# Mamba-2 scan and ELU feed-forward on one Trainium2 core: words of y in shared buffers and two groups sooner, decays begun at a stage's end, copies and B's loads elsewhere

## Chip, core and metric

One NeuronCore of a Trainium2 chip runs the kernel in one launch. The metric is the device time in microseconds (us). Before the change: 357.75 us, the median of three runs (357.48 to 358.91).

The core has five engines that run their own queues in order: TensorE (PE, with its weight loads as PEld), VectorE (DVE), ScalarE (ACT), GpSimd (POOL) and SyncE (SP, which here issues nearly all DMAs). They meet through semaphores, and each buffer is waited for by whoever takes it next.

## What is computed

A state-space scan over 4 batches, 8 heads and 768 tokens (head dimension 32, state 16), then a feed-forward layer with ELU (256 to 2048 to 256) on its output.

```python
for c in range(nc):                       # chunks of 32 tokens
    cum = np.cumsum(la, axis=-1)          # la = log(clip(a, 1e-6, 1))
    L = np.exp(cum[:, :, :, None] - cum[:, :, None, :]) * causal
    M = np.einsum('bhin,bhjn->bhij', Cc, Bc) * L
    y[:, :, sl] = (np.einsum('bhij,bhjd->bhid', M, xc)
                   + np.einsum('bhin,bhnd->bhid', Cc, state) * np.exp(cum)[..., None])
    decay_from_j = np.exp(cum[:, :, -1:] - cum)
    Bx = np.einsum('bhjn,bhjd->bhjnd', Bc, xc) * decay_from_j[:, :, :, None, None]
    state = np.exp(np.sum(la, axis=-1))[:, :, None, None] * state + np.sum(Bx, axis=2)
x = y.transpose(0, 2, 1, 3).reshape(3072, 256)
h = x @ w_in                              # 3072 x 2048
out = np.where(h > 0, h, np.exp(np.minimum(h, 0)) - 1) @ w_out
```

## The kernel before, in words

**Tiling.** The 3072 tokens are twelve groups of 256 (`NP` = 12). From group 2 on, groups are handled in pairs n, n+1 with n = 2, 4, 6, 8, 10, so that one matmul has 512 columns. The scan uses chunks of 64 tokens and works on the pair m = n+2 while the feed-forward works on pair n.

**Words.** From the pair 2 on, the products are made from operands split in two words each: for `h`, w1 and w0 of w and y1 and y0 of y, with a third product of sums (`both`), so three passes of two matmuls (`l1_words`, L828). After them ACT scales `both` into `e` (L834), DVE joins the two (L841), ACT makes ELU's two steps (`begin_end`, L848 and L849), and DVE the result g (`end_words`, L855). For the second product each tile of g is split by a job of three steps: ACT the high word (L909), DVE the low one (L910), POOL their sum (L887), begun, continued and ended by `first_of_jobs`, `second_of_jobs` and `third_of_jobs`. The second product itself (`second`, L968) takes six matmuls of 256 columns per step. For the first pairs it is `l2` (L873), whose result is copied by ACT into `ob` and written out.

**Stages.** The last loops run over n = 4, 6, 8, 10 ("stages"), each over k = 0 to 15, the sixteen column groups of w_in. In a step k the order written out by hand is: job to begin, `l1_words(n, k)`, loading of the words of w for k+4 (k even, `load_words`, 768 KB), the scan's part of that step (`stage_scan`), ELU, the jobs' third step, then so many steps of `second(n-2)` as the list after `l2s` says. Ahead of them lies a loop over j = 8 to 15 (i = j-8) for pair 2, in which the words of w and w_out are also made (`words_of_w`, `low_of_w`, `words_of_out`, `low_of_out`) and pair 4 is scanned.

**The scan in a stage.** For the pair m: `decay_sums` (POOL, L531, one instruction on 128x1024) adds the running sums, `decay_exps` (ACT, L538, two halves), `decay_mask` (POOL, L544, two selects for each half); `turn_part` transposes C and B (DVE), masks heads (part 2, POOL L476) and scales (part 3, POOL L459); `scaled` weights B's tokens (POOL, L423); at k = 9 to 13 come `scores`, `weigh`, `sums`, `states`, `across` and `inside`, and `inside` copies y from PSUM into yT (L687 on DVE, L689 on ACT), once for t = 0 and once for t = 1. SP loads x at k = 2 (`load_x`), B and C for two pairs ahead at k = 6 and 7 (`load_bc`), the decays' sums at k = 11 (`spread_cum`) and B by tokens at k = 12 (`load_b`).

**The end of a stage.** At k = 15 `l1_words` also makes the next pair's words of y: `high_of_y` (y1, one half on ACT L789, one on DVE L793), `low_of_y` (y0, two DVE instructions L802) and `both_of_y` (two, L812). y1 and y0 have one buffer each. The next stage's first group takes the passes on y1 and y0 first and the one on `both` last.

**Buffers.** `big` (4 KB a partition, 26 of them) holds the raw weights, g, the words of g, w and w_out. `small` (2 KB, 17 of them) holds the merged weights w_in and w_out, low words, `ob` and `eo`. A new tile takes the buffer that was freed longest ago in the order of the program, and waits until its last reader is done. PSUM has seven banks for all (`p_a`) and one more (`p_o`), in which `l2` and part of the scan accumulate.

Of the kernel before, what the change touches and what calls it, by code (L numbers as in the profile page):

```python
# [17 lines left out]
P = 128  # L18
# [6 lines left out]
BIG, SMALL = 26, 17  # L25
# [8 lines left out]
def kernel(  # L34
# [627 lines left out]
    def inside(y, *ns, t=None):  # L662

        for t in range(2) if t is None else (t,):
# [16 lines left out]
            for v in range(2):  # L681
                k = shift(n, v)
                for at in (0, k) if k else (0,):
                    count, src = P - k, (at + k) % P
                    to, src = out[at:at + count, :, :, Q * v:Q * v + Q], y[t][v][src:src + count]
                    if t and n == 1:
                        nc.vector.tensor_copy(to, src)  # L687
                    else:
                        nc.scalar.copy(out=to, in_=src)  # L689
# [96 lines left out]
    def high_of_y(n):  # L786
        y = yT[n // 2].rearrange("p k b u i -> p k (b u i)")
        y1 = conv.tile([P, KC, 2 * BLK], F32R, tag="y1", name="y1", bufs=1)
# [8 lines left out]
    def low_of_y(n):  # L797
        y = yT[n // 2].rearrange("p k b u i -> p k (b u i)")
        y1, = y_words[n]
        y0 = conv.tile([P, KC, 2 * BLK], F32R, tag="y0", name="y0", bufs=1)  # L800
# [16 lines left out]
    def l1_words(n, m, ahead=None):  # L817
# [13 lines left out]
        if ahead:  # L831
            high_of_y(ahead)
# [5 lines left out]
        if ahead:  # L838
            low_of_y(ahead)
            both_of_y(ahead)  # L840
        nc.vector.scalar_tensor_tensor(  # L841
            out=high, in0=high, scalar=WORD - 1.0, in1=e, op0=ALU.mult, op1=ALU.add)
        second_of_jobs()
        late.append((n, m, high, e))
# [20 lines left out]
    def l2(n, j, half=None):  # L865
# [11 lines left out]
        if j == MC // 2 - 1 and half != 0:  # L877
            ob = small([P, 2, DM], F32, "ob")
# [12 lines left out]
    def words_of_out(i):  # L891
# [3 lines left out]
        out_words[i] = small([P, 2, DM], F32R, "o_low"), words[:, 0], words[:, 1]  # L895
# [5 lines left out]
    def low_of_out(i):  # L901
        sub(out_words[i][0], pieces[DF // CW + i][0], out_words[i][1].bitcast(F32))
# [306 lines left out]
    for j in range(2 * DIRECT):  # L1209
# [44 lines left out]
        if j == 6:  # L1254
            words_of_w(5)
            low_of_w(5)
            keep_words(4)
    for j in range(8, 16):
# [48 lines left out]
        if i == 6:  # L1307
            decay_sums(6)
# [10 lines left out]
    def stage_scan(n, k):  # L1319
# [9 lines left out]
        if 0 < k < 5:  # L1329
            decay_exps(m + (k > 2), (k - 1) % 2)  # L1330
        if k == 0:
            decay_sums(m + 1)
        if 2 < k < 7:
            decay_mask(m + (k > 4), (k - 3) % 2)
        if k in (2, 7):
            turn_part(m + (k > 2), 2)
        if k in (8, 9):
            scaled(m + k - 8, nc.gpsimd)
        if k == 10:
            turn_part(m, 3)  # L1340
            turn_part(m + 1, 3)
        if k in (6, 7) and m + 2 < NP:
            load_bc(m + k - 4)
        if k in (11, 12) and m + 2 < NP:
            for to in (m + 2, m + 3):
                (spread_cum if k < 12 else load_b)(to)
        if k == 14 and m + 2 < NP:
            decay_sums(m + 2)

    for n in range(4, NP, 2):  # L1350
# [12 lines left out]
        for k in range(16):  # L1363
# [6 lines left out]
            l1_words(n, k, m if k == 15 else None)  # L1370
# [13 lines left out]
            l2s((2 - (n == 4 and k < 1), 2, 2, 2, 2, 2, 2, 2, 2, 2, 2, 2, 2, 1, 1, 0)[k])  # L1384
# [16 lines left out]
        if m:  # L1401
            l2s(2)
# [48 lines left out]
```

## Time and profile before

| what | value |
|---|---|
| median of 3 runs | 357.75 us |
| profiled execution, its own time | 359.41 us |
| its span in the profile | 357.70 us |
| mean granted TensorE clock | 0.995 |
| stage n = 4: first L828 to that of n = 6 | 119.76 to 174.90 us |
| stage n = 6 | 174.90 to 229.91 us |
| stage n = 8 | 229.91 to 284.07 us |
| stage n = 10 | 284.07 us to about 331 us |

The page of the profile lists the busy time of each engine, the chain of work that ended last, and groups of instructions with the idle time ahead of them. The table of waits has, for each pair of waiting line and line waited for, the total in us, how often, and the longest. A row of the timeline has its start, its length, the engine and line, the operation, output and inputs, how many were merged (x), and in brackets how long the engine idled before it and what released it. The ends of matmuls are modelled, so the distance between starts is the better measure of TensorE's pace.

### The profile page before, as it was taken

The page shows a single profiled execution, that of the slowest core. Times are in us where ns is not written, and L with a number is a line of the kernel's source. Part 1 is how long each engine was busy: PE and PEld are TensorE (multiplying, and loading weights), DVE is VectorE, ACT ScalarE, POOL GpSimd, SP SyncE. Part 2 cuts the span into 40 slices and gives each one's busy share as a digit, 9 for nine tenths or more (in the row PEclk, how much of TensorE's full clock was granted, in tenths as well). Part 3 has the DMA queues.
Part 4 walks back from the last instruction along what each step waited for, and adds up shares of the span by engine and source line. Part 5 has one row for each costly group of instructions (what it writes and reads, how often), then busy time and mean ns, then how long its engine had stood idle before and what let it go on. Part 6 is the DMA issues. An engine that isn't in the chain of part 4 may idle for free.

```text
span 357.7 us, 9627 instructions
## 1 busy us (share of the span) xinstructions
PE 342.2 (96%) x3742; PEld 290.0 (81%) x3742; DVE 282.3 (79%) x502; ACT 262.7 (73%) x542; POOL 213.9 (60%) x242
## 2 busy tenths in 40 slices
PE   8889999996999999998999999999999999999996
PEld 6569888884888788886688788788788789999996
DVE  3898989886697867794799987699887587998951
ACT  4698989694858898765689856689866688997601
POOL 5553554538757795976178977368986144876100
PEclk9999999999899999999999999999999999999999
DMA  8899989372468494538138669329364035250001
GB/s 140 206 226 188 283 159 254 71 152 89 164 122 307 186 267 166 197 91 173 75 101 203 216 229 218 100 79 242 150 225 161 2 107 200 88 198 0 32 0 59
DMA packets 82950, 54.79 MB, mean 153 GB/s; under 512 B 59033, under 2 KB 68569, under 8 KB 82905
## 3 DMA queue, kind: packets, MB, share of 16 engines
q1 hardware_dynamic: 80728, 53.98, 54.3%
q8 instruction: 29, 0.48, 0.6%
q10 hardware_dynamic: 2176, 0.20, 0.5%
q14 instruction: 17, 0.13, 0.1%
HBM read 44.53 MB, written 9.63 MB: 151 GB/s over the span
## 4 chain that ended last, share of the span: by engine, by line
PE 57%; DVE 15%; ACT 9%; POOL 9%; issue 5%; SPq 2%; DMA 2%; DVEq 0%; POOLq 0%; ACTq 0%
PE ps_o L968 11%; PE ps_h L828 10%; PE ps_o L873 9%; PE ps_h L711 9%; PE ps_w L828 5%; PE ps_both L968 5%; DVE ps_h L841 4%; DVE g_low L910 3%; POOL g_words L887 3%; POOL L L544 3%; PE ps_y L672 2%; ACT e L849 2%; ACT e L848 2%; DVE y L802 2%; DMA w<-in_moe_w_in_dram 2%
## 5 line engine op out<-in xcount | busy, mean ns | idle before, releaser
L887 POOL TENSOR_TENSOR g_words<-g_words,g_low 128x512 fp32r<-128x512 f32 x62 | 84.8, 1371 | 65.8 <-ACT e L848 40.4
L968 PE MATMUL ps_o<-o_words,g_words 128*128 128x256 f32 x448 | 84.3, 285 | 1.1 <-POOL g_words L887 0.8
L968 PEld LDWEIGHTS ps_o<-o_words,g_words 128*128 128x128 f32 x448 | 72.5, 190 | 8.7 <-POOL g_words L887 4.4
L848 ACT ACTIVATE e<-ps_h 128x512 f32<-128x512 f32 x72 | 43.0, 598 | 37.4 <-DVE ps_h L841 37.3
L855 DVE SCALAR_TENSOR_TENSOR g<-e,ps_h 128x512 f32<-128x512 f32 x72 | 49.3, 684 | 20.7 <-ACT e L849 18.2
L841 DVE SCALAR_TENSOR_TENSOR ps_h<-ps_h,e 128x512 f32<-128x512 f32 x72 | 49.9, 694 | 18.5 <-ACT e L834 15.7
L968 PE MATMUL ps_o<-o_low,g_low 128*128 128x256 f32 x224 | 63.2, 282 | 0.0
L910 DVE SCALAR_TENSOR_TENSOR g_low<-g_words,g 128x512 fp32r<-128x512 f32 x72 | 61.3, 857 | 0.0
L828 PE MATMUL ps_w<-y_both,w_words 128*128 128x512 f32 x144 | 50.7, 429 | 0.7
L873 PE MATMUL ps_o<-w_out,g 128*128 128x256 f32 x192 | 47.2, 391 | 3.4 <-ACT ob L879 3.4
L834 ACT ACTIVATE e<-ps_w 128x512 f32<-128x512 f32 x72 | 42.1, 585 | 7.7 <-PE ps_w L828 7.1
L711 PE MATMUL ps_h<-yT,w_in 128*128 128x256 f32 (+1 forms) x208 | 45.2, 368 | 2.3 <-POOL w_in L254 2.3
L849 ACT ACTIVATE e<-e 128x512 f32<-128x512 f32 x72 | 45.5, 632 | 2.3
L828 PE MATMUL ps_h<-y,w 128*128 128x512 f32 x144 | 46.2, 397 | 0.8 <-DVE y L802 0.4
L828 PE MATMUL ps_h<-y,w_words 128*128 128x512 f32 x144 | 45.9, 400 | 0.7 <-DVE M L586 0.7
L873 PEld LDWEIGHTS ps_o<-w_out,g 128*128 128x128 f32 x192 | 37.0, 195 | 9.4 <-ACT ob L879 3.7
L909 ACT ACTIVATE g_words<-g 128x512 fp32r<-128x512 f32 x72 | 43.6, 623 | 0.0
L711 PEld LDWEIGHTS ps_h<-yT,w_in 128*128 128x128 f32 x208 | 36.3, 190 | 8.3 <-POOL w_in L254 3.4
L968 PEld LDWEIGHTS ps_o<-o_low,g_low 128*128 128x128 f32 x224 | 42.6, 190 | 0.0
L828 PEld LDWEIGHTS ps_h<-y,w 128*128 128x128 f32 x144 | 27.0, 188 | 9.4 <-DVE y L802 2.7
L828 PEld LDWEIGHTS ps_h<-y,w_words 128*128 128x128 f32 x144 | 26.2, 188 | 9.3 <-PE ps_w L828 1.9
L828 PEld LDWEIGHTS ps_w<-y_both,w_words 128*128 128x128 f32 x144 | 23.8, 192 | 5.5 <-DVE y_both L812 3.3
(135 smaller groups left out, 547.7 us busy)
## 6 DMA issues: line engine op xcount, KB each, us to landing
w_words<-w_kept SPq DMA_DIRECT2D x28, 512.0 KB
w<-w_kept SPq DMA_DIRECT2D x28, 256.0 KB
L<-flat SPq DMA_DIRECT2D x20, 256.0 KB
w<-in_moe_w_out_dram SPq DMA_DIRECT2D x8, 512.0 KB
w_kept<-w_words SPq DMA_DIRECT2D x8, 512.0 KB
w<-in_moe_w_in_dram SPq DMA_DIRECT2D x7, 512.0 KB
xr<-in_x_dram SPq DMA_DIRECT2D x24, 128.0 KB
out_dram<-eo SPq DMA_DIRECT2D x18, 128.0 KB
```

Of the source, the lines that this page charges most:

```text
L711: nc.tensor.matmul(out=ps[:, j, toks], lhsT=w_in[i][:, k, j * P:(j + 1) * P], rhs=yT[n // 2][:, k, n % 2].rearrange("p u i -> p (u i)")[:, ...
L828: nc.tensor.matmul(out=ps, lhsT=lhs[:, k], rhs=rhs[:, k], start=k == 0 and lhs is not w0, stop=k == KC - 1 and lhs is not w1)
L834: nc.scalar.activation(e, both, ACT.Copy, scale=WORD)
L841: nc.vector.scalar_tensor_tensor(out=high, in0=high, scalar=WORD - 1.0, in1=e, op0=ALU.mult, op1=ALU.add)
L848: nc.scalar.activation(e, high, ACT.Relu, scale=-1.0)
L849: nc.scalar.activation(e, e, ACT.Exp, scale=-1.0)
L855: nc.vector.scalar_tensor_tensor(out=g_tile(n, m // 2)[:, m % 2].rearrange("p b i -> p (b i)"), in0=e, scalar=1.0, in1=h, op0=ALU.subtract ...
L873: nc.tensor.matmul(out=o_of[n][:, ts], lhsT=g_of[n // 2, j][:, m % 2, n % 2, ts * P:(ts + 1) * P], rhs=w_out[j][:, m % 2], start=(m == 0 a ...
L887: nc.gpsimd.tensor_tensor(out=out, in0=in0, in1=in1, op=ALU.subtract)
L909: yield nc.scalar.activation(words[:, 0], g, ACT.Copy, scale=NEAR / WORD)
L910: yield nc.vector.scalar_tensor_tensor(out=low, in0=words[:, 0].bitcast(F32), scalar=WORD, in1=g, op0=ALU.mult, op1=ALU.subtract)
L968: nc.tensor.matmul(out=ps, lhsT=lhs, rhs=rhs, start=lhs is both_g and first > 0 or lhs is g1 and first > 1, stop=last and lhs is not g1, s ...
```

## The change

y1 and y0 take buffers from `big`, which has 28 instead of 26. `high_of_y` and `low_of_y` for the next pair are made at k = 14 instead of 15, `both_of_y` at k = 15 behind L841. `decay_sums` of the next pair is issued at k = 13 and 14, the first `decay_exps` at k = 15, the other three at k = 0 to 2 of the next stage, `decay_mask` at k = 0 to 3; the masks of heads at k = 4 and 5, `scaled` at 7 and 8. `load_b` goes from k = 12 to k = 3 and 5 of the stage that uses it. From pair 6 on the t = 1 copies of `inside` are made by DVE. `ob` is taken from `big`, and `o_low` is taken when it is written. One step of `second` moves from k = 12 to the stage's end.

```diff
-BIG, SMALL = 26, 17
+BIG, SMALL = 28, 17
...
-                    if t and n == 1:
+                    if t and (n == 1 or n > 4):
                         nc.vector.tensor_copy(to, src)
                     else:
                         nc.scalar.copy(out=to, in_=src)
...
-        y1 = conv.tile([P, KC, 2 * BLK], F32R, tag="y1", name="y1", bufs=1)
+        y1 = big([P, KC, 2 * BLK], F32R, "y1")
...
-        y0 = conv.tile([P, KC, 2 * BLK], F32R, tag="y0", name="y0", bufs=1)
+        y0 = big([P, KC, 2 * BLK], F32R, "y0")
...
-        if ahead:
-            high_of_y(ahead)
         e = ffn.tile([P, 2 * BLK], F32, tag="e", name="e", bufs=2)
         nc.scalar.activation(e, both, ACT.Copy, scale=WORD)
         first_of_jobs()
         if late:
             end_words()
-        if ahead:
-            low_of_y(ahead)
-            both_of_y(ahead)
+        if ahead and m == MC - 2:
+            high_of_y(ahead)
         nc.vector.scalar_tensor_tensor(
             out=high, in0=high, scalar=WORD - 1.0, in1=e, op0=ALU.mult, op1=ALU.add)
+        if ahead and m == MC - 1:
+            both_of_y(ahead)
         second_of_jobs()
+        if ahead and m == MC - 2:
+            low_of_y(ahead)
...
-            ob = small([P, 2, DM], F32, "ob")
+            ob = big([P, 2, 2, DM], F32, "ob")[:, 0]
...
-        out_words[i] = small([P, 2, DM], F32R, "o_low"), words[:, 0], words[:, 1]
+        out_words[i] = None, words[:, 0], words[:, 1]
...
     def low_of_out(i):
+        out_words[i] = small([P, 2, DM], F32R, "o_low"), *out_words[i][1:]
...
+    def begin_decays(m, k):
+
+        if k < 15:
+            decay_sums(m + k - 13)
+        else:
+            decay_exps(m, 0)
+
...
-        if i == 6:
-            decay_sums(6)
+        if i > 4:
+            begin_decays(6, i + 8)
...
-        if 0 < k < 5:
-            decay_exps(m + (k > 2), (k - 1) % 2)
-        if k == 0:
-            decay_sums(m + 1)
-        if 2 < k < 7:
-            decay_mask(m + (k > 4), (k - 3) % 2)
-        if k in (2, 7):
-            turn_part(m + (k > 2), 2)
-        if k in (8, 9):
-            scaled(m + k - 8, nc.gpsimd)
+        if k < 3:
+            decay_exps(m + (k > 0), (k + 1) % 2)
+        if k < 4:
+            decay_mask(m + (k > 1), k % 2)
+        if k in (4, 5):
+            turn_part(m + k - 4, 2)
+        if k in (7, 8):
+            scaled(m + k - 7, nc.gpsimd)
...
+        if k in (3, 5) and n > 4:
+            load_b(m + (k > 3))
...
-        if k in (11, 12) and m + 2 < NP:
+        if k == 11 and m + 2 < NP:
             for to in (m + 2, m + 3):
-                (spread_cum if k < 12 else load_b)(to)
-        if k == 14 and m + 2 < NP:
-            decay_sums(m + 2)
+                spread_cum(to)
+        if k > 12 and m + 2 < NP:
+            begin_decays(m + 2, k)
...
-            l1_words(n, k, m if k == 15 else None)
+            l1_words(n, k, m)
...
-            l2s((2 - (n == 4 and k < 1), 2, 2, 2, 2, 2, 2, 2, 2, 2, 2, 2, 2, 1, 1, 0)[k])
+            l2s((2 - (n == 4 and k < 1), 2, 2, 2, 2, 2, 2, 2, 2, 2, 2, 2, 1, 1, 1, 0)[k])
...
         if m:
-            l2s(2)
+            l2s(3)
```

## Prediction

> **What bounds the kernel now.** I read the page first. TensorE is busy 96% of the 357.7 us span, so what counts is where it stands still or runs slowly; the other engines matter only through that. The table of waits says who makes it stand.
>
> ```profile
> PE   342.2 (96%) x3742; PEld 290.0 (81%) x3742; DVE 282.3 (79%) x502; ACT 262.7 (73%) x542; POOL 213.9 (60%) x242
> ...
> ACT ob L879 <- POOL w L887: 5.0, 1, 5.0
> ...
> PEld ps_o L968 <- POOL g_words L887: 4.4, 9, 0.8
> ...
> PE ps_o L873 <- ACT ob L879: 3.4, 1, 3.4
> ```
>
> One wait of 3.4 us stands out, and its cause is another wait: ScalarE's output copy waited 5.0 us for POOL. The timeline shows it, and the table by stretches the clock (its last three columns: granted clock, DMA share, GB/s).
>
> ```profile
> 83.14 0.61 ACT L767 ACTIVATE w_words<-w_in 128x512 fp32r<-128x512 f32 x1
> 87.31 1.40 POOL L887 TENSOR_TENSOR w<-w_in,w_words 128x256 fp32r<-128x256 f32 x2
> 88.75 0.59 ACT L879 COPY ob<-ps_o 128x512 f32<-128x512 f32 x1 [4.99 <-POOL w L887]
> ...
> 85.90:89.50 3.60, 0.20 (x2) 0.11 (x2) 0.08 (x1) 0.75 (x2) 2.67 (x4) 1.00 0.19 73
> 89.60:92.90 3.30, 3.30 (x9) 2.59 (x9) 2.17 (x4) 3.02 (x9) 1.31 (x2) 0.50 0.79 290
> ```
>
> ob needs no data of POOL's L887. It needs a "small" buffer, and the one that comes free is w_in[5]'s, whose last reader is that L887. TensorE idles, and is then granted half its clock for 3.3 us. Three further places, from the timeline of TensorE: the end of a stage (first two rows), a stop put down to issue (third), and POOL late with g_words (fourth).
>
> ```profile
> 175.98 1.10 PE L828 MATMUL ps_h<-y,w 128*128 128x512 f32 x2 [0.45 <-DVE y L802]
> 177.18 1.10 PE L828 MATMUL ps_w<-y_both,w_words 128*128 128x512 f32 x2
> ...
> 169.21 0.71 PE L672 MATMUL ps_y<-M,xr 64*32 64x64 f32 x48 [1.74 <-issue]
> ...
> 202.69 0.51 PE L968 MATMUL ps_o<-o_words,g_words 128*128 128x256 f32 x2 [0.41 <-POOL g_words L887]
> ```
>
> **1. ob to the big buffers.** The two L828 matmuls at 85.08 are followed by L873 4.31 us later, undisturbed 0.45 (93.83 to 94.28); 0.2 of that is another wait, so 3.7 lost. The eight L873 at half clock take 3.08 (89.39 to 92.47) against 1.54 (94.28 to 95.82), the next pair 0.89 against 0.65: 1.8 more. Together 5.5. The new ob needs a free big buffer: at that point 12 g tiles, two word tiles of w and y's two hold 16 of 28, and the last raw weight was freed by POOL's L254 at 80.95. So ob can run when its matmuls end, near 84.3, 0.59 long, before TensorE asks for the bank near 85.5. What is late next: the low words of w (POOL, done 88.71) are wanted at 95.82 - 5.5 = 90.3; POOL's mask for the scores was held up by the same ACT queue, would end near 88.7 + 1.4 + 1.35 = 91.5 and is wanted at 97.5 - 5.5 = 92.0. Both fit, narrowly. Bounds 3.7 to 5.5; I take **-5.4**, as the half clock follows the idle stretch directly. The two later ob waited for TensorE at most 0.3: nothing.
> [...]
>
> **2. B's loads.** Now four loads of 64 KB are issued at k = 12 of a stage: SyncE spends 7.09 us on them from 160.02. TensorE's stop of 1.74 us lies at 167.47. In the DMA records a 16 KB packet of the instruction queue q8 starts at 166.92 and ends at 167.87, amid the loads' 64-byte packets (164.9 to 169). I read the stop as code that came late behind them. Moved to k = 3 and 5 of the next stage the loads leave this place; the same place of the two later stages shows no stop. Bounds 0 to 1.9; taken **-1.4**.
> The price: at k = 3 and 5 SyncE's queue is full. In stage n = 6 it issues from 183.17 to 207.5 almost without a pause, x's four loads alone 6.37 us (188.43), then the words of w for k = 8 at 194.9, whose packets are in by about 199.2 while TensorE begins k = 8 at 200.74: 1.5 us spare. B's two loads in front add 1.0 to 3.5 us (pairs of 1.01 and 1.14 at 99.15 and 102.90; 7.09 for four). Stage n = 8 has some 3 us spare. scaled() on POOL, at k = 7 and 8, wants B near then. Cost 0 to 2 in n = 6, 0 to 1 in n = 8; taken **+0.7**. n = 4 keeps its early loads.
>
> **3. Decays begun at the stage's end.** Per stage POOL does the same: two sums (L531, 1.95 each), eight selects (L544), ctm, scaling. The selects move from k = 3 to 6 to k = 0 to 3. A pair of selects and a job make 1.84 + 1.30 = 3.14 us against TensorE's 2.82 a step (stage n = 10: k = 3 begins at 294.04, k = 4 at 296.86), so four such steps lag 1.3. Before, with ctm behind them, this ended in late g_words: L968 comes 0.70 and 1.02 after the last L828 pair instead of 0.46 at 199.20 and 202.69, and 0.72, 0.72, 1.02 in n = 8: 0.80 + 1.08 = 1.9 us. Now the lag begins where the third filler group of part 4 (0.72) gives POOL time, and ctm follows a step later. Bounds 0 to 1.9; taken **-1.5**. The exps (0.62 on ACT) move to k = 15 to 2: ACT idles 2.5 to 3.2 us there, so they are hidden.
>
> **4. y's words two groups sooner.** At the end of stage n = 4 the matmul pairs start at 174.90, 175.98, 177.18 and TensorE goes on at 178.12: 1.08, 1.20, 0.94 instead of 0.47 each, 1.8 lost; 1.1 each in n = 6 (pairs at 230.41 and 231.61) and n = 8. With y1 and y0 in own buffers no matmul must end first. But VectorE makes most of it, in order. In n = 6: L841 of k = 14 at 226.77, L910, L793, L855, two L802, two L812, done at 232.16, hardly a pause. After the change the t = 1 copies of inside come to it (three of about 0.4: TensorE's L672 ends near 224.9, so 224.95 to 226.2), then L855 of k = 13 that waited behind them, L793, L841, L910, two L802, L855, L841, two L812: 226.2 + 0.6 + 0.5 + 0.6 + 0.7 + 1.3 + 0.6 + 0.6 + 1.25 = 232.35. So y_both is ready no sooner; y1 and y0 are, by 1 us. Third filler group at the end: +0.72 there, but taken from k = 12, where it covers the wait for Sx (POOL L629 ends 220.99; the products L654 begin 220.49 now and would begin 219.77), so it gives nothing on balance. What stays is the first pair's wait: 0.6 in n = 4, 0.3 in n = 6 and n = 8. Bounds -0.6 to 4.0 of gain; taken **-1.2**. L841 of k = 15 now stands before y_both and is 1.2 sooner, so the banks and eo that hold TensorE 0.2 to 0.4 at k = 1 and 2 (waits on ACT L834, 1.3 in all, and DVE eo, 0.8) come sooner: **-0.6**.
>
> o_low allocated later and BIG 28 (26 and y's two): no instruction more, nothing.
>
> **Sum:** -5.4 - 1.4 + 0.7 - 1.5 - 1.2 - 0.6 = -9.4. The profiled execution took 359.41 (span 357.70, 1.71 around it), 1.66 above the median of 357.75; 350.0 for it, so **348.3** as median.
>
> **Rivals.**
> A. Every loss shown goes and nothing new comes: 5.5 + 1.9 + 1.9 + 4.0 + 1.1 = 14.4, 343.4 us. For: TensorE is the bound in between. Against: part 4's VectorE row. Chance 0.12.
> B. Only ob's gain lasts, 5.4 less about 1.5 for SyncE and for Sx: 353.9; with the stop gone too 352.5. For: VectorE is busy 19.45 of 20 us from 180 to 200. Chance 0.12.
> C. POOL against VectorE. VectorE's L910 took 1.94 instead of 0.68 at 180.87, beside POOL's L531 (180.32 to 182.27). The sums now run at k = 13 and 14, where L910 and L802 stand on the path to y_both: up to 1.26 later at three ends, 3.8: 352.1. Against: L531 at 223.08 met VectorE idle. Chance 0.08.
> [...]
> D. Slower: B's loads stretch as at 160.02 (7.1 us for four) in front of the words of w in n = 6 and n = 8. TensorE would wait 7.1 - 1.5 and 7.1 - 3, 9.7, and after two such stops run 2 x 1.8 at half clock: 13.3, so 348.3 - 0.7 + 13.3 = 360.9. It decides once the loads issue over 6 us late in both stages. Against: x's loads there took 1.6 each at 128 KB. Chance 0.06.
> E. ob finds no free buffer or a like wait takes its place: 353.7. Chance 0.04.
>
> **Chances.** Forecast 0.56 (own range 345.5 to 351), A 0.12, B 0.12, C 0.08, D 0.06, E 0.04, no change 0.02. 0.5% (1.8 us) is about what a measurement here can tell: faster 0.92, same 0.02, slower 0.06. The range from 344.0 to 354.0 leaves out D, no change and most of A, 0.2 in all.
>
> **What would show it.** ob right behind its L873, no granted clock of 0.50 near 86 to 93: part 1. No issue wait in inside: part 2; an L828 that waits for DMA at k = 8 shows its price. No PE wait on g_words at k = 7 to 9: part 3. The pair on y_both still waiting for L812 at a stage's start: part 4; if it does not wait, A. A stall of TensorE over 3 us anywhere else would make the forecast wrong.

## The result and the profile after

The changed kernel takes **354.35 us** (median of 7 runs, 353.45 to 356.24) against 358.27 us for the kernel before in the same rounds: 3.9 us less, ratio 0.9897 [0.9872, 0.9923]. A second set gave 353.5 against 358.16, ratio 0.9872 [0.9842, 0.9903]. The forecast was 348.3 (344.0 to 354.0), so the sign was right and the gain less than half of it. The profiled executions took 359.41 and 353.79 us, 5.6 us apart; the one of before is 1.1 us above its median, so what follows adds up to more than the medians differ by. In the changed kernel L841, L834, L910, L887, L968 and L873 are L838, L832, L912, L888, L970 and L874.

First the table of waits (waiting line, line waited for, us in total, times, longest), of the changed kernel and then of the kernel before:

```profile
PEld ps_w L828 <- DVE y_both L812: 6.2, 8, 1.4
...
PEld ps_y L654 <- POOL Sx L629: 2.7, 7, 0.5
...
PEld ps_y L672 <- issue: 1.3, 1, 1.3
...
PEld ps_o L970 <- POOL g_words L888: 1.2, 3, 0.5
```

```profile
PEld ps_w L828 <- DVE y_both L812: 3.3, 8, 0.4
...
PEld ps_h L828 <- ACT e L834: 1.3, 3, 0.4
...
PEld ps_h L828 <- DVE eo L977: 0.8, 2, 0.4
```

The wait for ob is gone and that for g_words fell from 4.4 to 1.2. That for y_both, which part 4 was about, rose from 3.3 (longest 0.4) to 6.2 (longest 1.4), and the one put down to issue is still there. Those of L828 for ScalarE's L834 and for eo are gone. Next the timeline where ob is copied, and the table by stretches there (last columns: granted clock, DMA share, GB/s):

```profile
84.23 0.59 ACT L880 COPY ob<-ps_o 128x512 f32<-128x512 f32 x1 [0.60 <-PE ps_o L874]
```

```profile
85.90:89.50 3.60, 3.60 (x18) 3.07 (x17) 3.00 (x5) 3.32 (x10) 3.45 (x5) 1.00 0.81 292
89.60:92.90 3.30, 3.30 (x72) 2.63 (x74) 3.30 (x5) 2.91 (x6) 3.15 (x5) 1.00 0.35 120
```

ob runs as soon as its L874 end, TensorE works through both stretches, and the clock stays whole. TensorE's other losses, from its timeline:

```profile
172.08 1.10 PE L828 MATMUL ps_w<-y_both,w_words 128*128 128x512 f32 x2 [0.93 <-DVE y_both L812]
...
219.01 0.38 PE L672 MATMUL ps_y<-M,xr 64*32 64x64 f32 x18 [1.15 <-issue]
...
227.13 1.10 PE L828 MATMUL ps_w<-y_both,w_words 128*128 128x512 f32 x2 [0.98 <-DVE y_both L812]
```

The pair on y_both starts 1.55 us after the pair ahead of it (170.53 to 172.08) instead of 0.47; n = 8 and n = 10 are alike. The stop by issue has left inside of n = 4 and come up in inside of n = 6.

The starts of the first L828 of each step tell where the time went. Counted from that of n = 2, which came at 83.97 and 83.84, the changed kernel's lead over the kernel before is:

| stretch | us gained (+) or given back (-) |
|---|---|
| n = 2, to its last two steps, which run as one | +5.21 |
| from there to k = 1 of n = 4 | -1.83 |
| k = 1 to 12 of n = 4 | 0 |
| k = 12 of n = 4 to k = 1 of n = 6 | +1.58 (stop gone 1.95, the rest -0.37) |
| k = 1 to 12 of n = 6, and of n = 8 | +1.80 and +1.80 |
| k = 12 of n = 6 to k = 1 of n = 8 | -2.40 (new stop -1.36, the rest -1.04) |
| k = 12 of n = 8 to k = 1 of n = 10 | -1.04 |
| n = 10 and the end | +0.37 |
| sum | +5.49 |

### The profile page after: what moved, and what is told of

It reads as the page before. It is cut to its first block, busy times and chain, and to the rows that moved or that the text cites. A ratio compares the mean times of both kernels' runs of the same rounds, so it can differ in the third digit from the quotient of the medians.

```text
span 352.1 us, 9631 instructions
## 1 busy us (share of the span) xinstructions
PE 338.1 (96%) x3742; PEld 290.4 (82%) x3742; DVE 290.3 (82%) x511; ACT 259.4 (74%) x533; POOL 215.2 (61%) x242
## 4 chain that ended last, share of the span: by engine, by line
PE 66%; DVE 12%; POOL 8%; ACT 4%; issue 3%; DMA 3%; SPq 3%; POOLq 0%; DVEq 0%; ACTq 0%
PE ps_o L970 16%; PE ps_h L828 12%; PE ps_h L711 11%; PE ps_o L874 9%; PE ps_w L828 6%; PE ps_both L970 5%; POOL g_words L888 3%; DVE ps_h L838 2%; PE ps_y L672 2%; DVE g_low L912 2%; DMA w<-in_moe_w_in_dram 2%; POOL L L544 2%; PE ps_g L577 2%; DVE g L856 2%; DVE M L586 1%
## 5 line engine op out<-in xcount | busy, mean ns | idle before, releaser
L888 POOL TENSOR_TENSOR g_words<-g_words,g_low 128x512 fp32r<-128x512 f32 x62 | 83.1, 1345 | 65.4 <-ACT e L849 30.1
L970 PE MATMUL ps_o<-o_words,g_words 128*128 128x256 f32 x448 | 83.6, 284 | 0.2
L970 PEld LDWEIGHTS ps_o<-o_words,g_words 128*128 128x128 f32 x448 | 72.9, 190 | 6.0 <-POOL g_words L888 1.2
L849 ACT ACTIVATE e<-ps_h 128x512 f32<-128x512 f32 x72 | 43.1, 599 | 38.3 <-DVE ps_h L838 37.8
L970 PE MATMUL ps_o<-o_low,g_low 128*128 128x256 f32 x224 | 63.3, 283 | 0.0
L912 DVE SCALAR_TENSOR_TENSOR g_low<-g_words,g 128x512 fp32r<-128x512 f32 x72 | 63.2, 884 | 0.0
L856 DVE SCALAR_TENSOR_TENSOR g<-e,ps_h 128x512 f32<-128x512 f32 x72 | 49.2, 684 | 16.0 <-ACT e L850 12.7
L838 DVE SCALAR_TENSOR_TENSOR ps_h<-ps_h,e 128x512 f32<-128x512 f32 x72 | 49.9, 693 | 4.5 <-ACT e L832 2.4
L828 PE MATMUL ps_w<-y_both,w_words 128*128 128x512 f32 x144 | 50.5, 427 | 3.3 <-DVE y_both L812 2.8
L832 ACT ACTIVATE e<-ps_w 128x512 f32<-128x512 f32 x72 | 42.2, 586 | 13.0 <-PE ps_w L828 12.6
L828 PE MATMUL ps_h<-y,w_words 128*128 128x512 f32 x144 | 45.3, 395 | 1.5 <-ACT y L791 0.8
L874 PE MATMUL ps_o<-w_out,g 128*128 128x256 f32 x192 | 45.5, 380 | 0.0
L828 PE MATMUL ps_h<-y,w 128*128 128x512 f32 x144 | 45.3, 393 | 0.2
L970 PEld LDWEIGHTS ps_o<-o_low,g_low 128*128 128x128 f32 x224 | 42.7, 191 | 0.0
L874 PEld LDWEIGHTS ps_o<-w_out,g 128*128 128x128 f32 x192 | 36.1, 190 | 5.4
L828 PEld LDWEIGHTS ps_h<-y,w_words 128*128 128x128 f32 x144 | 26.5, 188 | 8.9 <-PE ps_w L828 1.9
L828 PEld LDWEIGHTS ps_h<-y,w 128*128 128x128 f32 x144 | 27.0, 188 | 7.5 <-issue 0.9
L828 PEld LDWEIGHTS ps_w<-y_both,w_words 128*128 128x128 f32 x144 | 23.6, 191 | 8.1 <-DVE y_both L812 6.2
```

Of the source, the lines that this page charges most:

```text
L828: nc.tensor.matmul(out=ps, lhsT=lhs[:, k], rhs=rhs[:, k], start=k == 0 and lhs is not w0, stop=k == KC - 1 and lhs is not w1)
L832: nc.scalar.activation(e, both, ACT.Copy, scale=WORD)
L838: nc.vector.scalar_tensor_tensor(out=high, in0=high, scalar=WORD - 1.0, in1=e, op0=ALU.mult, op1=ALU.add)
L849: nc.scalar.activation(e, high, ACT.Relu, scale=-1.0)
L856: nc.vector.scalar_tensor_tensor(out=g_tile(n, m // 2)[:, m % 2].rearrange("p b i -> p (b i)"), in0=e, scalar=1.0, in1=h, op0=ALU.subtract ...
L874: nc.tensor.matmul(out=o_of[n][:, ts], lhsT=g_of[n // 2, j][:, m % 2, n % 2, ts * P:(ts + 1) * P], rhs=w_out[j][:, m % 2], start=(m == 0 a ...
```

## The experiments

Each ran in five rounds beside the kernel before. Five sets shared a chip and its runs of before: e1 to e4; e5 to e8; c_after, e9, e10 and e12; e13, c_halves and e14; e15 and e16. Between sets the ratio is what to compare. An interval is some 0.003 to either side, about 1 us.

| run | us | ratio to before [95%] |
|---|---|---|
| changed kernel, c_after | 354.35, 353.5 | 0.9897 [0.9872, 0.9923], 0.9872 [0.9842, 0.9903] |
| e1_ob_alone | 352.89 | 0.9861 [0.9833, 0.9889] |
| e2_copies_act | 352.59 | 0.9852 [0.9825, 0.988] |
| e3_decays_as_before | 352.86 | 0.9859 [0.9832, 0.9886] |
| e4_words_late | 351.23 | 0.9815 [0.9789, 0.9842] |
| e5_b_at_12 | 352.31 | 0.9828 [0.9805, 0.985] |
| e6_filler | 355.42 | 0.9905 [0.9867, 0.9942] |
| e7_words_late_mixed | 350.55 | 0.9784 [0.9758, 0.9811] |
| e8_halves, c_halves | 346.77, 346.56 | 0.9689 [0.9653, 0.9725], 0.9682 [0.9651, 0.9712] |
| e9_both_first | 352.34 | 0.9839 [0.9809, 0.987] |
| e10_jobs_first | 350.21 | 0.9779 [0.9749, 0.981] |
| e12_load_after_inside | 350.66 | 0.9789 [0.976, 0.9819] |
| e13_words_by_act | 351.77 | 0.9812 [0.9783, 0.9841] |
| e14_second_sum_later | 348.85 | 0.9741 [0.9712, 0.9771] |
| e15_low_first | 351.61 | 0.9809 [0.9773, 0.9845] |
| e16_low_and_both_first | 352.24 | 0.9816 [0.9779, 0.9854] |

The expectations' "Theory C" is the prediction's rival C, POOL against VectorE. The changed kernel once more:

> The changed kernel itself once more, beside the others on their chip, with a second profile. If its loss at the three stage starts is of the program (VectorE's order), the waits for y_both stand there again with 1.1 + 0.37 us each; the stops in inside and the end of stage n = 2 may differ by 1 to 2 us from run to run. Time 353.5 to 354.9 us, 0.989 of before.

The waits for y_both stand there again, 1.09 to 1.15 and 0.37 us at each of three starts, the end of n = 2 loses 1.9 and the stop 1.28.

**One line alone.** The kernel before with:

```diff
-            ob = small([P, 2, DM], F32, "ob")
+            ob = big([P, 2, 2, DM], F32, "ob")[:, 0]
```

> The kernel before with one line changed: ob comes from the big buffers. My term for it was -5.4 us. Theory 1 (the wait for POOL and the half clock after it are the whole of this term, and nothing downstream takes any of it back): 358.3 - 5.4 = 352.9 us, so better than the whole change (354.35). Rival (the end of stage n = 2 is bound by VectorE and ScalarE there, whatever POOL does, and takes back the 1.7 us that it took back in the changed kernel, where the lead fell from 5.2 to 3.5 us between 87 and 119 us): 354.8. The two are told apart by the start of the first L828 of n = 4, k = 1: 117.5 or 119.2 us.

Measured 352.89, as theory 1 said (to a hundredth by luck: the interval is 1 us). From the first L828 of n = 2 to that of k = 1 in n = 4 it took 33.49 us, before 38.70, changed kernel 35.32: nothing is given back at the end of n = 2. (That L828 came at 115.70, not 117.5, as this run was 1.8 us sooner from its first L828 of n = 2 on.) So **this line brings as much as the whole change**, within the intervals, and all the rest together is worth nothing that they show.

**Part 4 undone** (y's words at k = 15 in the old order, copies and filler as before, own buffers kept; two of the places changed):

```diff
-            l1_words(n, k, m)
+            l1_words(n, k, m if k == 15 else None)
...
-                    if t and (n == 1 or n > 4):
+                    if t and n == 1:
```

> The changed kernel with y's words made at k = 15 again in the order of the kernel before, the t = 1 copies on ScalarE and the filler groups where they were; y1 and y0 keep their own big buffers. My term for this part was -1.2 and -0.6: by it the kernel loses 1.8, 356.1 us. Theory 1 (the part costs about 0.8 us at each of three stage ends, since both_of_y now stands behind L838 of k = 15 and the copies on VectorE): 354.35 - 2.4 = 352.0 us. Rival (the ends are late for POOL's sums beside VectorE, not for the order): 354.3, no change.

Measured 351.23, 2 to 3 us less by the ratios: part 4 costs what theory 1 said, and my own term is refuted. The pair on y_both waits 0.37 + 0.37 us there instead of 1.10 + 0.37. In the profiles, stops by issue left aside, each of the three ends (k = 12 to k = 1 of the next stage) is 1.3 us shorter and the middles (k = 1 to 12) of n = 6 and n = 8 are 0.5 longer each. Another 1.0 us came at the end of n = 2, which this edit leaves alone, so part of the difference is not its own.

**Its pieces: copies, order, low words.** In turn: the t = 1 copies to ScalarE; on top of that both_of_y ahead of L838; and, in the changed kernel itself, two lines put the other way round:

```diff
+        if ahead and m == MC - 2:
+            low_of_y(ahead)
         second_of_jobs()
-        if ahead and m == MC - 2:
-            low_of_y(ahead)
```

> The changed kernel with the t = 1 copies of inside back on ScalarE; all else of the change stays. Theory 1 (the stage ends are bound by VectorE's queue in order): in n = 6 the three copies took VectorE from 219.40 to 220.71, with L856 of k = 13 waiting behind them; on ScalarE, which stood idle 2.65 us until 220.09, they cost nothing there, VectorE is 1.3 us sooner at each of three ends, y_both too: 354.35 - 3 x 1.0 to 1.3 = 350.5 to 351.4. Rival (VectorE's instructions at the end are long because POOL runs beside them, and ScalarE's queue is late there as well): no change within 0.5 us, or up to 1.3 us slower, as the copies then stand in front of ScalarE's L832 of k = 14 and L789.

> The kernel of e2_copies_act (the change with the t = 1 copies on ScalarE) with both_of_y of k = 15 in front of L838 of k = 15, no longer behind it. Theory 1 (both_of_y is late by what VectorE has in front of it): the first wait for y_both of 0.61 us at each of three stage starts shrinks by the 0.6 us of one L838 less the 0.24 us to the 0.37 us that a wait on the second half keeps, so by 0.24 to 0.6: 352.6 - 0.7 to 1.8 = 350.8 to 351.9. Rival (L838 of k = 15 is wanted as early as y_both, by the banks): 352.6, with the waits of L828 at k = 1 instead.

> The changed kernel with low_of_y (two L802) of k = 14 in front of the job's L912, no longer behind it; the number of VectorE's instructions ahead of y_both is the same. Theory C at its second place (POOL's L888, which needs L912 and runs beside L802, locks VectorE for 1.1 us): the two L802 take 1.3 us and no longer 2.39, y_both comes up to 1.1 us sooner, and the first wait for it (1.10 us) shrinks to 0 to 0.5 at three stage starts: 353.9 - 1.8 to 3.3 = 350.6 to 352.1. Rival (the lock goes over to L856 or L838 behind it, and the sum of VectorE's work is the same): 353.9, with an L856 or L838 of 1.8 us.

In e2 the first wait fell from 1.10 to 0.61 us at all three starts, in e9 to under 0.1, with the second half's 0.37 left. Theory 1 is right in kind but too large for e2 (0.5, not 1.0 to 1.3), and in the time neither shows beyond the interval: 352.59, and 352.34, above the 350.8 to 351.9 expected. The profiled e9 lost 2.7 us at the end of n = 2 and 1.62 in a stop, against 1.9 and 1.28 in c_after. But in e9 the rival came true as well: with L838 behind both_of_y, L828 waits at k = 1 for ScalarE's L832 (0.42 to 0.43 us in n = 6, 8 and 10; in e2 there is no such wait) and L970 longer for g_words at k = 3 and 4. The middles of n = 6 and n = 8 take 34.76 and 34.50 us, 34.00 and 33.84 in e2, and that is as much as the starts gained. e15 gave 351.61, inside theory C's 350.6 to 352.1. VectorE and then POOL in the changed kernel, and the same in e15_low_first:

```profile
221.69 0.69 DVE L838 SCALAR_TENSOR_TENSOR ps_h<-ps_h,e 128x512 f32<-128x512 f32 x1
222.29 0.68 DVE L912 SCALAR_TENSOR_TENSOR g_low<-g_words,g 128x512 fp32r<-128x512 f32 x1
222.89 2.39 DVE L802 SCALAR_TENSOR_TENSOR y<-y,yT 128x512 fp32r<-128x512 f32 x2
225.20 0.68 DVE L856 SCALAR_TENSOR_TENSOR g<-e,ps_h 128x512 f32<-128x512 f32 x1
225.79 0.69 DVE L838 SCALAR_TENSOR_TENSOR ps_h<-ps_h,e 128x512 f32<-128x512 f32 x1
226.40 1.28 DVE L812 SCALAR_TENSOR_TENSOR y_both<-y,yT 128x512 fp32r<-128x512 f32 x2
```

```profile
223.14 1.59 POOL L888 TENSOR_TENSOR g_words<-g_words,g_low 128x512 fp32r<-128x512 f32 x1 [3.24 <-PE ps_h L828]
```

```profile
221.19 1.28 DVE L802 SCALAR_TENSOR_TENSOR y<-y,yT 128x512 fp32r<-128x512 f32 x2
222.39 0.68 DVE L912 SCALAR_TENSOR_TENSOR g_low<-g_words,g 128x512 fp32r<-128x512 f32 x1
223.00 0.68 DVE L856 SCALAR_TENSOR_TENSOR g<-e,ps_h 128x512 f32<-128x512 f32 x1
223.59 0.69 DVE L838 SCALAR_TENSOR_TENSOR ps_h<-ps_h,e 128x512 f32<-128x512 f32 x1
224.19 1.50 DVE L812 SCALAR_TENSOR_TENSOR y_both<-y,yT 128x512 fp32r<-128x512 f32 x2
```

```profile
223.25 1.30 POOL L888 TENSOR_TENSOR g_words<-g_words,g_low 128x512 fp32r<-128x512 f32 x1 [4.44 <-DVE g_low L912]
```

The reader is to see POOL's start against VectorE's. In the changed kernel POOL subtracts what L912 has just made, and the two L802 beside it take 2.39 us; put ahead of L912 they take 1.28. In e15 POOL runs beside L856 and L838 instead, each of which has one input in PSUM, and these keep their 0.68 and 0.69; only the L812 at its end is held up, by 0.2. TensorE's first wait shrank from 1.10 to 0.22, 0.26 and 0.27, and the stretches from k = 12 to k = 1 of the next stage, stops left aside, by 0.9, 0.9 and 0.8 us. The lock, in the expectations' word, is here no more than this: the longer time that a VectorE instruction with both inputs in SBUF took beside one of POOL (2.39 for 1.28 us here, 1.94 for 0.68 in the row of rival C).

**All three at once.** e9_both_first with low_of_y ahead of second_of_jobs as well.

> The kernel of e9_both_first (the change with the t = 1 copies on ScalarE and both_of_y in front of L838 of k = 15) with the two L802 in front of L912 as well. Theory (the three things together put y_both late: the copies 0.5, L838 0.6, the lock 1.1 us at each end): the last wait of 0.37 us at three starts goes: 352.3 - 1.1 = 351.2, and L828 waits for y_both nowhere in n = 6, 8 and 10. Rival (the words of g are late in turn, as in e8_halves, where L931 stood behind them): 352.3 or slower, with a wait for g_words at k = 15 or k = 0.

At the starts of n = 6, 8 and 10 L828 loses at most 0.16 us to y_both, nearly as the theory said; yet 352.24, as in the rival. Something does become late in turn, though not at the steps that the rival named: as in e9, L828 waits for ScalarE's L832 at k = 1 (0.17, 0.42 and 0.41 us) and L970 for g_words at k = 3 to 5 (0.33 to 0.53 us). The middles of n = 6 and n = 8 take 34.48 and 34.61 us, 34.02 and 33.87 in e15. Its profile also has two stops by issue in inside, 1.56 and 1.65 us, the first followed by half clock.

**Filler.** The changed kernel with the groups of L970 as before (two at k = 12, two at the end).

> The changed kernel with the filler groups of L970 where the kernel before has them (two at k = 12, two at the stage's end); B's loads stay at k = 3 and 5. Theory 2 of the stop (a place in TensorE's instruction stream decides, and the filler moves it): the stop comes after the 1983rd matmul again (0.9 to 2.0 us) and shrinks to 0.5 or nothing after the 2615th. Theory 1 (B's loads decide): none in n = 4. Time: the waits for Sx in L654 (0.43, 0.40, 0.53) go, the stage ends lose 0.72 of cover at three places, and what the third group covers there shows as longer waits for y_both: theory 2 and full cover lost 354.35 - 1.36 + 1.4 - 1.2 + 3 x 0.72 = 355.3; if the group covers nothing there, 353.2.

355.42, the first figure, but by luck: the stop after the 1983rd matmul was only 0.44 and that after the 2615th 1.16, so the sizes expected of theory 2 were wrong, and a cost that neither theory had came in. The profiled execution had half its clock from 171.47 to 174.88, where the first of the longer waits for y_both ends. Five of the six executions had a granted clock of 0.985 to 0.995 and took 353.68 to 356.98 us; the one at 1.000 took 352.35. The first wait for y_both became 1.57 us, about half a microsecond longer at each start, and the waits for Sx went: the third group does move cover from one place to another, as the prediction said.

**Decays as before** (sums, exps, selects, ctm and scaling back at their steps; B's loads not).

```diff
-        if i > 4:
-            begin_decays(6, i + 8)
+        if i == 6:
+            decay_sums(6)
...
```

> The changed kernel with the decays (sums, exps, selects, ctm and scaling) at the steps of the kernel before; B's loads stay at k = 3 and 5. Theory 1 (the earlier decays pay in the middle of the stages, where the changed kernel gained 1.78 us in n = 6 and in n = 8, and cost at the ends, where POOL's sums L531 run beside VectorE): the middles lose 2 x 1.8 = 3.6, the end of n = 2 gives 1.7 back and the three later ends up to 0.5 each: 354.35 + 3.6 - 1.7 - 0 to 1.5 = 354.8 to 356.3. Rival (POOL's sums lock nothing of weight, and the ends are late for VectorE's order alone): 357.9. Second rival (the middles gained by the third filler group and not by the decays): 352.6 or less.

Measured 352.86, near the second rival's figure: undoing part 3 costs nothing. Its reason does not hold, for with the filler groups as before (e6) the middles (k = 1 to 12) stay short, 33.92 and 34.08 us against 34.04 and 33.90 in the changed kernel and 35.83 and 35.70 before. In e3 they lost 0.5 us in n = 6 and 0.6 in n = 8, not 1.8 each; the end of n = 2 gave 1.7 back; the waits for y_both stayed 1.07 to 1.10, so POOL's sums do not make these ends late. The end of n = 2, VectorE and POOL, in the changed kernel and then in e3:

```profile
107.39 2.46 DVE L768 SCALAR_TENSOR_TENSOR w_words<-w_words,w_in 128x512 fp32r<-128x512 f32 x1
```

```profile
105.45 3.84 POOL L531 TENSOR_TENSOR L<-L,ncum 128x1024 f32<-128x1024 f32 x2
```

```profile
106.37 0.68 DVE L768 SCALAR_TENSOR_TENSOR w_words<-w_words,w_in 128x512 fp32r<-128x512 f32 x1
```

```profile
104.45 1.93 POOL L531 TENSOR_TENSOR L<-L,ncum 128x1024 f32<-128x1024 f32 x1
```

Beside two sums in a row L768 takes 2.46 us, 1.8 more than the 0.68 in e3, where the one sum ends just in time (at 106.38, and L768 starts at 106.37). Then ScalarE, which waits for VectorE's L838, is late with y1, and L828 of n = 4 with it. Against the kernel before, all nine kernels with the early sums there lose 0.7 to 2.7 us between these two steps, and the seven others (e1, e3, e7, e8, e10, e12, e14) 0.2 at most.

**B's loads back at k = 12.**

```diff
-        if k in (3, 5) and n > 4:
-            load_b(m + (k > 3))
...
-        if k == 11 and m + 2 < NP:
+        if k in (11, 12) and m + 2 < NP:
```

> The changed kernel with B's four loads back at k = 12 of a stage; all else of the change stays. My term for the move was -1.4 for TensorE's stop in inside and +0.7 for SyncE's queue. Theory 1 (the loads make the code late): the stop comes back in n = 4, 1.4 to 2.0 us, and that of n = 6 (1.36 us in the changed kernel) goes or stays: +0.6 to +2.0, 355 to 356.3 us. Theory 2 (the stop belongs to a place in TensorE's instruction stream: in the runs so far it comes after the 1983rd or the 2615th of TensorE's matmuls, the first with the filler groups as before, the second with those of the change, wherever B's loads are): the stop stays after the 2615th, none in n = 4, and the time is that of the changed kernel within 0.5 us: 353.9 to 354.9.

Both theories missed: 352.31 us, not slower and not the same but faster, ratio 0.9828 against 0.9897 and 0.9872 (the second interval overlaps a little), with stops of 0.26 and 0.42 instead of one of 1.36 (1.28 in c_after). The stop's place is fixed: in all profiles that have one it follows TensorE's matmul number 1983, or number 2615 or 2616 (counted from 0). What varies is its length, 0 to 2.2 us. In the DMA records it ends 1.2 to 1.6 us after the end of a 16 KB packet of the instruction queue, the code packet of the expectations (1.34 in the kernel before, where the packet ends at 167.87 and the stop at 169.21; 1.32 in the changed one, 217.69 and 219.01), and its length goes with that packet's start. For the second place the packet starts at matmul 2498 to 2506 where the words of w of k = 14 are issued behind it or by another queue (stop 0 to 0.5) and at 2538 to 2603 where SyncE has issued them ahead of it (stop 0.5 to 2.2). Why B's loads help is in SyncE's queue, in n = 6 of the kernel before and then of the changed kernel:

```profile
216.44 7.10 SPq L148 DMA_DIRECT2D b_tok<-in_B_dram  x4
223.65 0.52 SPq L757 DMA_DIRECT2D w_words<-w_kept  x1
```

```profile
208.43 0.54 SPq L757 DMA_DIRECT2D w_words<-w_kept  x1
...
212.90 0.32 SPq L757 DMA_DIRECT2D w_words<-w_kept  x1
```

Before, B's loads keep SyncE for 7.10 us and hold back the words of w of k = 14, and the code packet passes in the gap. Without them SyncE issues those words over 6 us ahead of TensorE's step k = 14 (219.32), and their traffic stands before the code. Two tests of that. The first moved the words of k = 12 behind inside in the program:

> The kernel of e7_words_late_mixed with the words of w that are loaded at k = 12 of a stage (768 KB) loaded behind inside instead, so that less traffic stands before the code packet that TensorE needs in inside. Theory 3 (TensorE reaches a fixed place of its stream 1.2 to 1.6 us or less after the code packet has landed, and that packet comes when the transfers in front of it are done): the packet comes sooner by up to the 2 us that these words take, and the stops of 1.70 and 2.16 us go in most executions: 350.55 - 1 to 3 = 347.5 to 349.5. Theory 2 (the packet is asked for at that place, whatever the traffic): the stops stay, 350.5. A price either way if the words come late for k = 0: an L828 that waits for DMA at the stage's start.

The stops stayed, 1.99 and 1.12, and the time too, 350.66. But the edit did not do what it was for: SyncE issued the same two loads at 209.21 and 212.28, as early as ever, since it waits for the last reader of the buffer (TensorE's L969 there) and not for the step in which the load is written. The second gave the words of k = 14 to ScalarE's queue, which is in step:

```diff
-                load_words((k // 2 + 2) % 8)
+                load_words((k // 2 + 2) % 8, nc.scalar if k == 14 else nc.sync)
```

> The changed kernel with the two loads of k = 14 of a stage (words of w, 768 KB) issued by ScalarE at k = 14 and no longer by SyncE. In the changed kernel SyncE issues them at 212.90, 6 us before TensorE's step k = 14 begins (219.32), and the code packet asked for near the 2500th matmul (215.4) begins at 216.8, when their traffic ends. Theory 3 (that traffic stands before the packet): the packet begins at once, the stop of 1.28 to 1.36 us after the 2615th matmul goes or falls under 0.5: 353.9 - 0.9 to 1.3 = 352.6 to 353.0. Rival (the packet is late whatever stands before it): the stop stays, 353.9, or more for two issues on ScalarE at three stage ends.

The code packet started at matmul 2498, the stop fell to 0.26 us, and the time to 351.77, below theory 3's 352.6 to 353.0. So for the second place the runs show the queueing: 0.26 us with those words out of SyncE's queue, 1.36 and 1.28 with them in it. For the first one (n = 4) they do not: six kernels with the old filler order, before among them, stop there for 0.4 to 2.0 us, but so do e5 (0.26) and e16 (1.56) with the new order, and e8, e10 and e14 with the old one do not. The length goes with the packet's start there as well (matmul 1866 to 1889: 0 to 0.26 us; 1898 to 1968: 0.4 to 2.0), but what sets that start stayed open: the words of k = 14 are issued behind the packet in the kernel before, which stops, and ahead of it in the changed kernel, which does not.

**Toward a better kernel.** e7 is e4 with the decays of pairs 6 and 7 as before, the others early.

> The kernel of e4_words_late with the decays of pair 6 and 7 (end of stage n = 2, stage n = 4) at the steps of the kernel before; the decays of the later pairs stay early. Theory C (POOL's sums and low words lock VectorE out at the end of n = 2, where e4_words_late lost 0.8 us and the changed kernel 1.8, and e3_decays_as_before only 0.1): 351.2 - 0.7 = 350.5 us, and no VectorE instruction L768 over 1.1 us between 105 and 113 us. Rival (that end is late for another reason, and varies from run to run): 351.2.

350.55, as expected; n = 2 ends without loss. e8 then makes y's words by halves, the t = 0 half right behind the first part of inside (one of the places changed):

```diff
                 inside(y, m, m + 1, t=0)
+                half_of_y(m, 0)
+                rest_of_half(m, 0)
```

> The kernel of e7_words_late_mixed with y's words made by halves: those of the t = 0 half (L793, L802, L812 of k = 0) right behind the first part of inside, those of the t = 1 half at k = 14; y_both in a big buffer. Theory 1 (VectorE's order at the stage's end is what TensorE waits for): the waits for y_both, 0.37 + 0.37 at each of three stage starts in e4_words_late, go: 350.5 - 2.2 = 348.3 us, and no L828 waits at n = 6, 8, 10. Rival (the three more big buffers in use make something else wait: the words of w, g or g_words): 350.5 or slower.

> The kernel of e8_halves once more, beside e14_second_sum_later on its chip: 346.3 to 347.2 us, 0.969 of before.

**346.77 and 346.56 us**, 11.7 and 11.6 us less than before and better than expected: TensorE waits for y_both at no stage start, and the stops nearly went as well (none in e8, one of 0.39 us in c_halves). In this kernel L849 is the changed kernel's L828, L831 and L834 make y0 and y_both, L931 is the job's low word, L907 POOL's subtraction, L989 `second`. What it still loses is a new wait of 1.2 to 1.4 us at the starts of n = 6 and n = 8, and its cause is once more the lock (TensorE at the start of n = 8, then VectorE at the end of n = 4, beside POOL's L531 of 161.45 to 163.57):

```profile
221.97 0.50 PE L989 MATMUL ps_o<-o_words,g_words 128*128 128x256 f32 x2 [1.21 <-POOL g_words L907]
```

```profile
161.80 2.31 DVE L831 SCALAR_TENSOR_TENSOR y<-y,yT 128x512 fp32r<-128x512 f32 x1
```

Two tries to take that away failed. One put L931 ahead of the t = 1 half, the other moved the second sum to k = 15:

> The kernel of e8_halves with the second instruction of the job (L931, g_low) in front of the t = 1 half of y's words at k = 14, no longer behind it. In e8_halves TensorE waits 1.20 us (167.79) and 1.36 us (220.38) for g_words, whose L931 stood behind two instructions of 0.6 us each. Theory 1 (VectorE's order): L931 is 1.2 us sooner, POOL's g_words too, and y_both 0.6 us later, about when TensorE asks for it: 346.8 - 1.5 to 2.4 = 344.4 to 345.3. Rival (POOL's L531 beside VectorE's L831, 2.31 us instead of 0.68, is what makes it late, and the 0.6 only moves the wait to y_both): 346.2 to 346.8.

> The kernel of e8_halves with the second of POOL's two sums (L531) at k = 15, behind the exps, and no longer at k = 14. Theory C (POOL's sum locks VectorE: L831 of the t = 0 half took 2.31 us beside it and 0.68 without): L831 falls to 0.7 us, all that VectorE does behind it comes 1.2 to 1.6 us sooner, and the waits for g_words of 1.20 and 1.36 us at the starts of n = 6 and n = 8 go: 346.8 - 1.2 to 2.6 = 344.2 to 345.6. Rival (the lock only moves to what VectorE does at k = 15 and at the next k = 0): 346.8, or up to 1 us slower.

350.21 and 348.85: 3.4 and 2.3 us slower. In e10 POOL's subtraction came sooner (167.62 to 169.20), and so ran beside the second half of y_both, which takes 1.77 us there and 0.68 in e8, and for which TensorE then waits 1.1 us at the starts of n = 6 and n = 8:

```profile
167.97 1.77 DVE L834 SCALAR_TENSOR_TENSOR y_both<-y,yT 128x512 fp32r<-128x512 f32 x1
```

In e14 L831 fell from 2.31 to 0.69 us and the wait at the stage's start went, as theory C said, which shows the lock to be its cause; but the sum, now at 168.29, stands in front of POOL's next subtraction, and TensorE waits 1.16 us for g_words one step later. Neither theory gave a time as long as that.

## Why the prediction was right or wrong

The two profiles give -5.5 us where the sum had -9.4. The end of n = 2 cost 1.8 that stood in no term, the ends of part 4 came out 3.6 worse (+2.4 for -1.2), and the middles of n = 6 and n = 8 were 1.5 better (-3.6 for -1.5 and -0.6); parts 1 and 2 nearly met their numbers, part 2 by luck.

**Part 1, -5.4: right.** 5.1 us from the first to the second step of n = 2, 4.8 in the medians of e1. Both halves of the term, the wait and the half clock, went together.

**Left out of the sum: the end of n = 2, +1.8.** The prediction counted POOL's sums as the same number at other steps and looked for their lock at three stage ends. It overlooked the fourth place to which the change takes them, i = 5 and 6 of the loop ahead, where words of w and w_out are made on VectorE. The mechanism was named as rival C, with a chance of 0.08 and at the wrong instructions.

**Part 2, -1.4 and +0.7: the reading failed.** "I read the stop as code that came late behind them" took one packet beside one transfer for a cause. At the second place the code packet does come late behind transfers (e13: a stop of 0.26 us instead of 1.36), but which ones is set by what SyncE issues next: with B's loads gone the words of k = 14 took their place (issued at 212.90, before at 223.65). Nor do B's loads decide in n = 4: e4, e6, e7 and e12 have none at k = 12 and stop there for 0.4 to 2.0 us. The stop of 1.95 us left n = 4 and one of 1.36 came in n = 6: net 0.6, near the 0.7 that was forecast, but by other stops than it thought, and e5 makes the move a loss. SyncE's price of 0.7 did not show: no L828 at k = 8 waits for DMA. Rival D fell with that.

**Part 3, -1.5: right in kind, too large.** The middles of n = 6 and n = 8 gained 3.6 us, 1.1 of it by the decays (in e3 L970 waits for g_words again, 0.3 to 0.9 us at k = 7 and 8). Part 4 undone costs about 0.5 in each of them too (e4), which leaves some 0.75 in each stage that neither brings back when undone alone. The step k = 2 is part of it (3.21 and 3.23 us before, 2.82 in the changed kernel, in e3 and in e4); the cause was not settled. With the end of n = 2 the part loses.

**Part 4, -1.2: the step that failed. Its -0.6 held in kind.** The ends came to +2.4 us (0.4, 1.0 and 1.0 at three of them). The prediction laid out VectorE's queue one instruction after the other, found y_both no later than before, at 232.35, and then counted a gain for the first pair. What it had wrong is a single addend: "two L802" at 1.3. They took 2.39 at all three ends, because POOL's subtraction of the job, which the new order sets free just then, runs at the same time (e15 takes it away, and they take 1.28). In the kernel before they had taken 1.55:

```profile
229.41 1.55 DVE L802 SCALAR_TENSOR_TENSOR y<-y,yT 128x512 fp32r<-128x512 f32 x2
```

The same addition with 2.39 gives 233.44, 6.35 us behind the start of k = 15 (227.09), and the changed kernel has it at 6.1; before it was 5.1. TensorE then asked in vain. Two lines changed places in e15, the lock on L802 went, and the ends came 0.9, 0.9 and 0.8 us shorter, about what the part had cost there. The gain of 1.2 hardly comes even so. L838 and the copies in front of y_both had their place in the sum, but a queue without slack turns each of them into TensorE's wait: 0.5 for the copies (e2) and 0.6 for L838 (e9). For L838 that buys something, which is the -0.6: in the changed kernel the waits for L834 and eo (1.3 and 0.8 us) are gone, and in e9, with L838 behind y_both, the one for ScalarE is back at k = 1. That the third group "gives nothing on balance" held: e6 shows it covering half a microsecond at one place and the waits for Sx (0.43, 0.40 and 0.53) open at the other.

**Rivals and range.** B gave nearly the result's figure (353.9, only ob's gain lasts), and e1 bears these words out. The figure was luck: of its two reasons Sx is a part (some 0.4 us at each of three ends) and SyncE's price did not show. C had the mechanism and the wrong places. A's losses all exist, but e8, not the change, removes most of them.

## What to carry to other kernels

When an instruction on VectorE with both inputs in SBUF moves, look up what POOL will be running at its new time, above all POOL's consumer of the instruction right ahead of it, and price it with the time that a trace shows for it beside POOL (here 2.39 us for two L802 that take 1.28 alone, 2.46 for an L768 of 0.68); instructions with an input in PSUM stood beside POOL's at no cost here (L856 and L838 in e15: 0.68 and 0.69 us). Here SyncE's queue did not wait for the step in which a load is written (e12: written behind inside, issued at 209.21 and 212.28 as ever): taking B's loads out brought the later words forward, from 223.65 to 212.90, and they stood before the code packet. And before several edits are judged together, try the one with the clear row alone: here one line was the whole gain.

## What the runs showed of the hardware that was not expected

TensorE stops at two fixed places of its stream, after matmul 1983 and after 2615 or 2616, and goes on 1.2 to 1.6 us after the end of a 16 KB packet of the instruction queue. Both lie in inside, where 64 matmuls of 64 columns take 0.86 us (the kernel before, from 165.43); the stops reach 2.2 us (2.16 in e7).

Half clock followed some of these stops. In e7_words_late_mixed TensorE stood still for 1.70 us from 161.1. Its table by stretches, with the columns PE busy, granted clock, DMA share, GB/s:

```profile
161.00:162.00 1.00, 0.32 (x17) 1.00 0.01 2
162.00:163.00 1.00, 0.20 (x25) 1.00 0.00 0
163.00:164.00 1.00, 1.00 (x49) 0.67 0.06 16
164.00:165.00 1.00, 1.00 (x4) 0.50 0.00 0
165.00:166.00 1.00, 1.00 (x4) 0.50 0.00 0
166.00:167.00 1.00, 1.00 (x6) 0.62 0.00 0
```

TensorE was busy for half a microsecond of the two, and then had half its clock for 3.41 us. The first stops of e12 (1.99 us) and e16 (1.56) did the same; those of 1.95 us in the kernel before and 2.16 us later in e7 did not. So the length of the stop alone does not decide, and the stop of 1.56 us already cost twice.

The clock records of the traces say more. Half clock stands ahead of the kernel's end in six profiles (before, e6, e7, e9, e12 and e16), all with a mean granted clock of 0.995. It lasts 3.41 us (89.56 to 92.97 in before, 171.47 to 174.88 in e6, 163.35 to 166.76 in e7), and in before it begins 81.92 us, 24 times as long, behind the point where the clock first became whole (7.64). Counted in steps of 3.41 us from the half clock of the same run, the stops of e7 (161.10 to 162.80) and e16 that half clock followed lie inside one step (e7: 159.93 to 163.35; e16: 160.77 to 164.18), and the two that it did not follow lie across a border (before: 167.25 to 169.21 across 168.06; e7: 217.13 to 219.30 across 217.96). TensorE was busy for some 57% of that step in e7 and 60% in e16. That is not the whole of it either, for e9's stop of 1.62 us lies inside one step (216.26 to 219.67) and no half clock followed. What decides there was not tried.
